# Pooled attention on one core: products with V in three blocks of 48 queries, two heads in the two halves of the PE's columns

## The chip, the cores and the metric

The kernel runs on one core of a Trainium2 chip (trn2). TensorE (PE) multiplies matrices, VectorE (DVE) and ScalarE (ACT) do elementwise work and move results out of the accumulators, GpSimd (POOL) does elementwise work in SBUF, and SyncE (SP) issues the DMAs. The metric is the device time of one execution in microseconds (us); the median of several runs is compared.

## The reference, cut to what matters

```python
q, k, v: (8 batches, 8 heads, 576 positions, 64)      # factor = 4, Sd = 576 // 4 = 144
q_d, k_d, v_d = mean over groups of 4 positions        # (8, 8, 144, 64)
out_d = softmax(q_d k_d^T / sqrt(64)) v_d              # pooled attention
out_up = np.repeat(out_d, 4, axis=2)
out_local = softmax over |i - j| < 4 of q k^T / sqrt(64), times v
x = (out_up + out_local), heads side by side           # (8, 576, 512)
xn = (x - mean) / sqrt(var + 1e-06) * g_ln
out = x + relu(xn @ w_ch1) @ w_ch2                     # 512 -> 2048 -> 512
```

The weights come as 64-bit floats and are read as pairs of 32-bit words.

## The kernel before, in words

One program holds both parts. The feed-forward part runs over 18 chunks of 256 tokens and, in each, over 8 pairs of 128-row blocks of the hidden layer: `up` (tile `h`, L1048), `relu` and `rest` (tiles `hh` on ACT, `hl` on DVE), `down` (tile `acc`, L1071). Each product is made of three passes over high and low parts of weights and activations. The weights are loaded by SP in 32 steps (tile `s`, L347 and L352: `s1_f` for the first matrix, `s2_f` for the second, f from 0 to 15) and split once into `hi` and `lo` by ACT (L359, L378) and DVE (tiles `cva`, L367 and L370, and `lo`, L383).

The attention part has 40 local windows (tiles `ls`, `lt`, `lv`; L587, L622, L643) and the pooled attention, which handles 4 heads at a time (`pooled_half`) and in it two pairs of heads (`pooled_pair`): 32 pairs in all, 4 of them in batch 0 (`own`, which gets its sums in another way) and 28 in the other batches. For one pair, both heads' queries stand in one block matrix `qbdg`, and the stages are: `turn_qk` (tile `gq`), `scores` (`gs`, L818, in three blocks of 48 queries a head), `largest`, `exps` (`ag`), `turn_a` (transposes into `gt`, L837, one for each half `kh` of the 144 keys), `turn_a_out` (ACT copies into `agt`, L847), `times_v` (products with V, tile `gv`, L854), `divided` (DVE, L861 to L871, tile `od`), and `keep` (DMA to the DRAM tile `ud`, L877), from where `load_up` (tile `up`, L917) reads it for the norm of the tokens. For the first seven windows and batch 0, other forms of some steps are used.

`times_v` makes, for each head h2 and each half qh of the 144 queries, a 72x65 block, summed over the two halves of the keys: 8 matrix products of 72 rows and 72 columns. A product of 32-bit floats is two passes on the PE, so that is 16 passes a pair, and 512 in all.

The order of everything is fixed before the program runs. `Plan.add` takes an engine, a duration, dependencies and a due time for every task; `Plan.order` plays the engines forward with these durations, and on each engine takes the task with the earliest due time among those that can start; the tasks are then written out in the order of their starts. Two kinds of numbers enter: the durations (1.04 for `times_v`) and the due times. `CHUNK` is the distance of chunks in due times, `chunk_at(c)` is `T0 + CHUNK * c` from the third chunk on, the times of windows and pooled pairs follow from it, and the weights are due at

```python
due = W0 + W_GAP * (f // 2) + 0.5 * (which - 1) + 1.0 * (f % 2)
```

or earlier, where a product that needs them is due earlier. Where the plan leaves the PE a gap in the first 150 us, `psa` writes extra products of the identity (L197) that only keep the PE running.

Of the kernel before, what the change touches and what calls it, by code (L numbers as in the profile page):

```python
# [9 lines left out]
F32 = mybir.dt.float32  # L10
# [4 lines left out]
ALU = mybir.AluOpType  # L15
# [7 lines left out]
class Plan:  # L23
# [14 lines left out]
    def add(self, eng, dur, fn, deps=(), due=0.0, take=(), give=(), lag=None, ahead=1e9, alt=None, kb=0):  # L38

        opts = {eng: (dur, fn, 0.0)}  # L40
        if alt is not None:
            opts[alt[0]] = alt[1:]
        t = SimpleNamespace(
            n=len(self.tasks), opts=opts, dur=dur, deps=[d for d in deps if d is not None],
            due=due, take=take, give=give, lag=lag, ahead=ahead, open=0.0, waits=0, eng=None, fn=None, kb=kb,
        )
        self.tasks.append(t)
        return t
# [91 lines left out]
def attention_then_ffn(  # L140
# [10 lines left out]
    nc = tc.nc  # L151

    P = 128
    B, H, S, D = q.shape
    DM = H * D
    w1, w2 = w1.bitcast(I32), w2.bitcast(I32)
    DFF = w1.shape[1] // 2
    FACTOR = 4
    SD = S // FACTOR
    GH = SD // 2  # L160
    GB = SD // 3
# [11 lines left out]
    NPE, NPB = 7, 1  # L173
# [11 lines left out]
    work = ctx.enter_context(tc.tile_pool(name="work", bufs=1))  # L185
    dram = ctx.enter_context(tc.tile_pool(name="dram", bufs=2, space=bass.MemoryType.DRAM))
    ps_a = ctx.enter_context(tc.tile_pool(name="ps_a", bufs=8, space=bass.MemoryType.PSUM))

    def unit(shape, name, dtype=F32, kind="u"):
        kind = kind if kind in SEP else "u"  # L190
        return work.tile(shape, dtype, tag=kind, bufs=SEP.get(kind, NU), name=name)

    def psa(name):
        p = ps_a.tile([P, 512], F32, tag="a", name=name)

        for _ in range(warm.pop() if warm else 0):
            nc.tensor.matmul(p[:, :P], lhsT=ident, rhs=ident, start=True, stop=True)  # L197
        return p
# [71 lines left out]

    T0 = 35
    C1 = 5
    CHUNK = 56
    PACE = CHUNK / NPR

    def chunk_at(c):
        return T0 + (C1 * c if c < 2 else CHUNK * c)

# [3 lines left out]
    def norm_at(n):  # L282
        c, j = divmod(n, TPC)
        return chunk_at(c) - 6.0 + 1.0 * j

    def window_of(n):
        b, s = divmod((n + 1) * P - 1, S)
        return b * NWIN + min(NWIN - 1, s // (2 * NQ))

    w_gap = CHUNK * S / T / NWIN  # L290
    w_base = min(norm_at(n) - 9.0 - window_of(n) * w_gap for n in range(2 * TPC, NTILE))
    g_base = min(norm_at(n) - 9.0 - (n * P + P - 1) // S * CHUNK * S / T for n in range(2 * TPC, NTILE))

# [5 lines left out]
    def pooled_at(b, pr):  # L299
        if b == 0:  # L300
            return norm_at(0) - B0G - B0G_GAP * (3 - pr)
        return g_base + b * CHUNK * S / T - (NPAIR - 1 - pr) * (CHUNK * S / T / NPAIR if b > 1 else G1)

# [2 lines left out]
    U_SPARE = 4  # L306
    NEARLY, EARLY = 2, 50
    G1, OFF0 = 6, 0.5
    W0, W_GAP = 40, 13
    plan = Plan({"u": NU, "stg": NSTG, "a": 8, **SEP}, {"a": 2, "u": U_SPARE})  # L310

    def rooms(*kinds):
# [6 lines left out]
    U, A, STG = (("u", 1),), (("a", 1),), (("stg", 1),)  # L319
    DMA, LAT, W_AHEAD, W_LAG = 0.5, 2.5, 40, 1.5  # L320
# [403 lines left out]
    ud, ud_done = {}, {}  # L724
    od, od_done = {}, []
# [8 lines left out]
    def pooled_half(b, hg):  # L734
# [41 lines left out]
        for pr in range(2):  # L776
            pooled_pair(b, hg, pr, x, ready)

    def pooled_pair(b, hg, pr, x, ready):
        add = plan.add  # L780
        i = 2 * b + hg
        due = pooled_at(b, 2 * hg + pr)
        y = SimpleNamespace(at={})
        own = b < NPB
        bd, vd = qbdg[pr], vds[hg]
# [47 lines left out]
        def turn_a(kh):  # L833
            y.pa = getattr(y, "pa", {})
            y.pa[kh] = psa(f"gt{i}_{pr}_{kh}")[:GH, : 2 * SD].rearrange("p (c h g) -> p c h g", c=3, h=2)
            for c in range(3):
                nc.tensor.transpose(  # L837
                    y.pa[kh][:, c].rearrange("p h g -> p (h g)"), y.a[:, c, kh * GH : (kh + 1) * GH],
                    ident[: 2 * GB, : 2 * GB],
                )  # L840

        def turn_a_out(kh):
            if own:
                y.at[kh] = unit([GH, 2, SD], f"agt{i}_{pr}_{kh}")
            else:
                y.at[kh] = work.tile([GH, 2, SD], F32, tag=f"agt{kh}", name=f"agt{i}_{pr}_{kh}")
            nc.scalar.copy(y.at[kh].rearrange("p h (c g) -> p c h g", c=3), y.pa[kh])  # L847

        def times_v():
            y.pv = psa(f"gv{i}_{pr}")[:GH, : 4 * (D + 1)].rearrange("p (q h e) -> p q h e", q=2, h=2)  # L850
            for h2 in range(2):
                for qh in range(2):
                    for kh in range(2):
                        nc.tensor.matmul(  # L854
                            y.pv[:, qh, h2], lhsT=y.at[kh][:, h2, qh * GH : (qh + 1) * GH],
                            rhs=vd[:, kh, 2 * pr + h2], start=kh == 0, stop=kh == 1,
                        )

        def divided():
            r = work.tile([GH, 2, 2], F32, tag="gr", bufs=4, name=f"gr{i}_{pr}")  # L860
            nc.vector.tensor_scalar(  # L861
                out=r, in0=y.pv[:, :, :, D], scalar1=1e-9, scalar2=float(FACTOR), op0=ALU.add, op1=ALU.mult
            )
            nc.vector.reciprocal(r, r)
            if b < NPB:
                if pr == 0:
                    od[hg] = unit([GH, 2, 2, 2 * D], f"od{i}")
                y.od = od[hg][:, :, pr].rearrange("p c (h d) -> p c h d", h=2)
            else:
                y.od = work.tile([GH, 2, 2, D], F32, tag="od", bufs=2, name=f"od{i}_{pr}")  # L870
            nc.vector.tensor_mul(y.od, y.pv[:, :, :, :D], r.unsqueeze(3).broadcast_to([GH, 2, 2, D]))  # L871
# [10 lines left out]
        if b < NPB:  # L882
            t = add("ACT", 0.43, arrange, ready["q"] + ready["k"] + [lastg.s[pr]], due - 8.0)
        else:
            t = add("PE", 0.25, turn_qk, ready["q"] + ready["k"], due - 8.0, take=A, give=(("u", 2),) if pr else ())
            t = add("ACT", 0.52, turn_qk_out, (t, lastg.s[pr]), due - 8.0, give=A)
        t = lastg.s[pr] = add(
            "PE", 0.73, scores, (t,), due - 6.0, take=A, give=(("u", 2),) if b < NPB and pr else ()
        )
        t = add("DVE", 0.7, largest, (t,), due - 5.0)  # L890
        ex = add("ACT", 0.79, exps, (t, None if own else lastg.t), due - 5.0, take=U if own else (), give=A)
        outs = []
        for kh in range(2):
            t = lastg.t = add("PE", 0.25, lambda kh=kh: turn_a(kh), (ex,), due - 3.0, take=A,
                                give=U if own and kh else ())
            outs.append(add("ACT", act(288), lambda kh=kh: turn_a_out(kh), (t, None if own else lastg.v), due - 3.0,
                            take=U if own else (), give=A))
        t = add("PE", 1.04, times_v, outs + ready["v"], due - 1.0, take=A, give=(("u", 2),) if own else ())
        lastg.v = lastg.vd[hg] = t
        t = add("DVE", 0.68, divided, (t,), due, take=U if b < NPB and pr == 0 else (), give=A)  # L900
        od_done.append(t)
        t = add("SP", 0.42, keep, (t,), due, lag=LAT)
        ud_done.setdefault(b, []).append(t)


# [265 lines left out]
```

## Time and profile before

| | |
|---|---|
| three runs | 1055.81, 1056.92, 1063.01 us; median 1056.92 |
| the profiled execution's own time | 1053.27 us |
| its span, first to last instruction | 1051.3 us |
| granted PE clock over the span | 0.995 |
| PE busy | 1034.3 us (98%) |
| DVE busy | 514.0 us (49%) |
| ACT busy | 309.8 us (29%) |
| POOL busy | 251.0 us (24%) |

A profile records one execution. Its durations are compared with its own time, 1053.27 us, of which 1.97 us lie outside the span. PE work is pipelined: the recorded durations of its passes overlap, so what a pass costs is read from one start to the next, not from the duration. "Granted clock" is the share of TensorE's full clock that was granted.

### The profile page before, as it was taken

Reading aid. Unit: us, or ns where it says so; the run is one execution under the profiler, and the core shown is the slowest. Engines: PE = TensorE matmul, PEld = TensorE weight load, DVE = VectorE, ACT = ScalarE, POOL = GpSimd, SP = SyncE. Lnnn points to the kernel's source line nnn. Section 1 sums busy time; section 2 is a strip of 40 time slices with the busy share of each in tenths; the row PEclk is TensorE's granted clock in tenths of the full one; section 3 lists DMA queues with packets and bytes.
Section 4 is the critical chain, followed back from the end, with each engine's and each line's share of the span. In section 5 each row is a group of like instructions: output and inputs, shape, how many; then the busy total and the mean of one; then the engine's idle time right before and its main releaser. Section 6 shows DMA issues by size and latency. Waiting matters only on the chain.

```text
span 1051.3 us, 24104 instructions
## 1 busy us (share of the span) xinstructions
PE 1034.3 (98%) x9450; PEld 928.9 (88%) x9450; DVE 514.0 (49%) x1301; ACT 309.8 (29%) x846; POOL 251.0 (24%) x272
## 2 busy tenths in 40 slices
PE   9999899999999999999999999999999999999998
PEld 8887798988899989989898989899989899888997
DVE  7799976343444435444434443544434444534211
ACT  6676533232212222221323222222221222221110
POOL 4213552214014320231404150141401300000000
PEclk9999999999999999999999999999999999999999
DMA  7897474434344534343434443253442443301000
GB/s 177 251 283 210 136 176 95 114 64 114 61 101 91 133 75 110 62 124 56 91 94 96 104 97 99 47 134 67 114 87 69 92 88 65 80 11 52 7 21 21
DMA packets 283702, 104.38 MB, mean 99 GB/s; under 512 B 229789, under 2 KB 270493, under 8 KB 283589
## 3 DMA queue, kind: packets, MB, share of 16 engines
q1 hardware_dynamic: 283589, 102.84, 40.8%
q8 instruction: 75, 1.23, 0.5%
q14 instruction: 38, 0.31, 0.1%
HBM read 82.58 MB, written 11.80 MB: 90 GB/s over the span
## 4 chain that ended last, share of the span: by engine, by line
PE 83%; DVE 6%; DMA 5%; SPq 2%; issue 1%; POOL 1%; ACT 1%; ACTq 0%; DVEq 0%; POOLq 0%
PE h L1048 34%; PE acc L1071 33%; PE gv L854 3%; DMA s<-in_moe_w_ch_dram 2%; PE gs L818 2%; PE lv L643 2%; PE ls L587 2%; DVE cva L370 2%; PE lt L622 1%; PE px L975 1%; PE gt L837 1%; DVE lo L383 1%; SPq L714 1%; DMA x<-xl 1%; DVE cva L367 1%
## 5 line engine op out<-in xcount | busy, mean ns | idle before, releaser
L1071 PE MATMUL acc<-hi,hl 128*128 128x512 f32 x576 | 237.2, 412 | 0.6 <-DVE hl L1059 0.5
L1071 PE MATMUL acc<-lo,hh 128*128 128x512 f32 x576 | 227.4, 395 | 0.0
L1071 PE MATMUL acc<-hi,hh 128*128 128x512 f32 x576 | 225.2, 391 | 0.0
L1059 DVE SCALAR_TENSOR_TENSOR hl<-h,hh 128x512 fp32r<-128x512 f32 x144 | 98.9, 687 | 250.7 <-ACT hh L1055 222.0
L1055 ACT ACTIVATE hh<-h 128x512 fp32r<-128x512 f32 x144 | 86.2, 599 | 430.3 <-PE h L1048 363.5
L1048 PE MATMUL h<-xh,lo 128*128 128x256 f32 x1152 | 193.6, 291 | 0.2 <-DVE lo L383 0.2
L1048 PE MATMUL h<-xh,hi 128*128 128x256 f32 x1152 | 185.2, 283 | 0.0
L1048 PE MATMUL h<-xlo,hi 128*128 128x256 f32 x1152 | 185.0, 283 | 0.0
L1048 PEld LDWEIGHTS h<-xh,lo 128*128 128x128 f32 x1152 | 169.0, 190 | 17.4 <-DVE lo L383 0.4
L1048 PEld LDWEIGHTS h<-xlo,hi 128*128 128x128 f32 x1152 | 158.9, 192 | 0.0
L1048 PEld LDWEIGHTS h<-xh,hi 128*128 128x128 f32 x1152 | 158.6, 191 | 0.0
L948 POOL TENSOR_TENSOR x<-x,up 128x512 f32<-128x512 f32 x32 | 41.2, 1287 | 386.3 <-DMA x<-xl 208.1
L1071 PEld LDWEIGHTS acc<-hi,hh 128*128 128x128 f32 x576 | 108.5, 188 | 25.0
L1071 PEld LDWEIGHTS acc<-hi,hl 128*128 128x128 f32 x576 | 109.2, 190 | 16.9 <-DVE hl L1059 1.2
L1071 PEld LDWEIGHTS acc<-lo,hh 128*128 128x128 f32 x576 | 109.5, 190 | 12.7 <-DVE lo L383 0.3
L982 ACT ACTIVATE xh<-px,gain 128x128 fp32r<-128x128 f32 x144 | 43.7, 372 | 72.7 <-PE px L975 42.4
L992 DVE SCALAR_TENSOR_TENSOR xlo<-px,gain,xh 128x128 fp32r<-128x128 f32 x144 | 43.1, 345 | 39.1 <-ACT xh L982 38.6
L1079 DVE SCALAR_TENSOR_TENSOR x<-acc,x 128x512 f32<-128x512 f32 x36 | 24.7, 689 | 39.8 <-PE acc L1071 39.8
L831 ACT ACTIVATE ag<-gs,gmx 96x144 f32<-96x144 f32 x96 | 29.0, 374 | 41.9 <-DVE gmx L823 34.4
L370 DVE SCALAR_TENSOR_TENSOR cva<-s,cva 128x256 int32<-128x256 int32 x64 | 40.0, 665 | 1.1
L854 PEld LDWEIGHTS gv<-vd,agt 72*72 72x72 f32 x512 | 37.1, 145 | 1.2
L854 PE MATMUL gv<-vd,agt 72*72 72x65 f32 x512 | 37.9, 228 | 0.0
(196 smaller groups left out, 1106.9 us busy)
## 6 DMA issues: line engine op xcount, KB each, us to landing
s<-in_moe_w_ch_dram SPq DMA_DIRECT2D x64, 256.0 KB
vwin<-in_v_dram SPq DMA_DIRECT2D x160, 64.0 KB
out_dram<-x SPq DMA_DIRECT2D x36, 256.0 KB
qr<-in_q_dram SPq DMA_DIRECT2D x264, 32.0 KB
kr<-in_k_dram SPq DMA_DIRECT2D x264, 32.0 KB
up<-ud SPq DMA_DIRECT2D x28, 256.0 KB
x<-xl SPq DMA_DIRECT2D x74, 42.0 KB
ud<-od SPq DMA_DIRECT2D x32, 72.0 KB
```

What stands on the lines that cost most here:

```text
L370: nc.vector.scalar_tensor_tensor(out=a, in0=x.raw[i].rearrange("p (n two) -> p n two", two=2)[:, :, 0], scalar=29, in1=a, op0=ALU.logical_ ...
L587: nc.tensor.matmul(x.ps[par][64 * h2 : 64 * h2 + 64, pr], lhsT=x.qt[hs, 2 * pr + h2], rhs=x.kt[hs, 2 * pr + h2], start=True, stop=True,)
L831: nc.scalar.activation(y.a[:, c], y.ps[:, c], AF.Exp, scale=POOLED_SCALE, bias=y.mx[:, c : c + 1])
L854: nc.tensor.matmul(y.pv[:, qh, h2], lhsT=y.at[kh][:, h2, qh * GH : (qh + 1) * GH], rhs=vd[:, kh, 2 * pr + h2], start=kh == 0, stop=kh == 1,)
L948: nc.gpsimd.tensor_add(xt[n], xt[n], x.up)
L982: nc.scalar.activation(xh[c][i][:, k, j * P : (j + 1) * P], pxt[n][:, kc], AF.Copy, scale=gain[:, kc : kc + 1])
L992: nc.vector.scalar_tensor_tensor(out=xlo[c][i][:, k, ts], in0=pxt[n][:, kc], scalar=gain[:, kc : kc + 1], in1=xh[c][i][:, k, ts].bitcast(F ...
L1048: nc.tensor.matmul(ph[c, p][:, fi], lhsT=wt[:, kc], rhs=xx[kc // 2][:, kc % 2], start=n == 0, stop=n == 3 * KC - 1)
L1055: nc.scalar.activation(hh[c, p], ph[c, p], AF.Relu)
L1059: nc.vector.scalar_tensor_tensor(out=hl[c, p].rearrange("p c t -> p (c t)"), in0=ph[c, p].rearrange("p c t -> p (c t)"), scalar=0.0, in1=h ...
L1071: nc.tensor.matmul(acc[c][j], lhsT=lt[:, fi, ts], rhs=rt, start=p == 0 and fi == 0 and n == 0, stop=p == NPR - 1 and fi == 1 and n == 2,)
L1079: nc.vector.scalar_tensor_tensor(out=x, in0=acc[c][j], scalar=1.0 + 2.0**-23, in1=x, op0=ALU.mult, op1=ALU.add)
```

## The change

For the 28 pairs of batches 1 to 7, `times_v_by_third` takes the place of `times_v`. The queries come in three blocks c of 48; head 0 of the pair gets output partitions 0 to 63 (48 of its own columns and 16 that belong to the next block and aren't used), head 1 partitions 64 to 111. `agt` is laid out flat, in the order in which the transposes leave it, so that a block's columns are contiguous. That makes 3 x 2 x 2 = 12 products of 64 or 48 columns a pair, in place of 8 of 72. `divided_by_third` handles 112 partitions x 192 elements in place of 72 x 256, and `keep_by_third` issues two DMAs in place of one, with rows of 64 elements in place of 128. Batch 0 stays as it was.

Three numbers of the plan change with it: the durations of these tasks (1.04 to 0.5 for the products, 0.68 to 0.6, 0.42 to 0.84), `CHUNK` from 56 to 55, and `W0` from 40 to 30. With these the plan writes out another order.

```diff
--- before.py
+++ after.py
@@ -270,7 +270,7 @@
 
     T0 = 35
     C1 = 5
-    CHUNK = 56
+    CHUNK = 55
     PACE = CHUNK / NPR
 
     def chunk_at(c):
@@ -306,7 +306,7 @@
     U_SPARE = 4
     NEARLY, EARLY = 2, 50
     G1, OFF0 = 6, 0.5
-    W0, W_GAP = 40, 13
+    W0, W_GAP = 30, 13
     plan = Plan({"u": NU, "stg": NSTG, "a": 8, **SEP}, {"a": 2, "u": U_SPARE})
 
     def rooms(*kinds):
@@ -842,9 +842,10 @@
         def turn_a_out(kh):
             if own:
                 y.at[kh] = unit([GH, 2, SD], f"agt{i}_{pr}_{kh}")
+                nc.scalar.copy(y.at[kh].rearrange("p h (c g) -> p c h g", c=3), y.pa[kh])
             else:
-                y.at[kh] = work.tile([GH, 2, SD], F32, tag=f"agt{kh}", name=f"agt{i}_{pr}_{kh}")
-            nc.scalar.copy(y.at[kh].rearrange("p h (c g) -> p c h g", c=3), y.pa[kh])
+                y.at[kh] = work.tile([GH, 6 * GB], F32, tag=f"agt{kh}", name=f"agt{i}_{pr}_{kh}")
+                nc.scalar.copy(y.at[kh], y.pa[kh].rearrange("p c h g -> p (c h g)"))
 
         def times_v():
             y.pv = psa(f"gv{i}_{pr}")[:GH, : 4 * (D + 1)].rearrange("p (q h e) -> p q h e", q=2, h=2)
@@ -855,6 +856,38 @@
                             y.pv[:, qh, h2], lhsT=y.at[kh][:, h2, qh * GH : (qh + 1) * GH],
                             rhs=vd[:, kh, 2 * pr + h2], start=kh == 0, stop=kh == 1,
                         )
+
+        def times_v_by_third():
+
+
+            y.pv = psa(f"gv{i}_{pr}")[: 64 + GB, : 3 * (D + 1)].rearrange("p (c e) -> p c e", c=3)
+            for c in range(3):
+                for kh in range(2):
+                    for h2 in range(2):
+                        m = GB if h2 else 64
+                        c0 = (2 * c + h2) * GB
+                        nc.tensor.matmul(
+                            y.pv[64 * h2 : 64 * h2 + m, c], lhsT=y.at[kh][:, c0 : c0 + m], rhs=vd[:, kh, 2 * pr + h2],
+                            start=kh == 0, stop=kh == 1,
+                        )
+
+        def divided_by_third():
+            r = work.tile([64 + GB, 3], F32, tag="gr", bufs=4, name=f"gr{i}_{pr}")
+            nc.vector.tensor_scalar(
+                out=r, in0=y.pv[:, :, D], scalar1=1e-9, scalar2=float(FACTOR), op0=ALU.add, op1=ALU.mult
+            )
+            nc.vector.reciprocal(r, r)
+            y.od = work.tile([64 + GB, 3, D], F32, tag="od", bufs=2, name=f"od{i}_{pr}")
+            nc.vector.tensor_mul(y.od, y.pv[:, :, :D], r.unsqueeze(2).broadcast_to([64 + GB, 3, D]))
+
+        def keep_by_third():
+            if b not in ud:
+                ud[b] = dram.tile([SD, DM], F32, tag="ud", name=f"ud{b}")
+            for h2 in range(2):
+                c0 = (4 * hg + 2 * pr + h2) * D
+                nc.sync.dma_start(
+                    ud[b].rearrange("(c g) e -> g c e", c=3)[:, :, c0 : c0 + D], y.od[64 * h2 : 64 * h2 + GB]
+                )
 
         def divided():
             r = work.tile([GH, 2, 2], F32, tag="gr", bufs=4, name=f"gr{i}_{pr}")
@@ -895,11 +928,11 @@
                                 give=U if own and kh else ())
             outs.append(add("ACT", act(288), lambda kh=kh: turn_a_out(kh), (t, None if own else lastg.v), due - 3.0,
                             take=U if own else (), give=A))
-        t = add("PE", 1.04, times_v, outs + ready["v"], due - 1.0, take=A, give=(("u", 2),) if own else ())
+        t = add("PE", 1.04 if own else 0.5, times_v if own else times_v_by_third, outs + ready["v"], due - 1.0, take=A, give=(("u", 2),) if own else ())
         lastg.v = lastg.vd[hg] = t
-        t = add("DVE", 0.68, divided, (t,), due, take=U if b < NPB and pr == 0 else (), give=A)
+        t = add("DVE", 0.6, divided if own else divided_by_third, (t,), due, take=U if b < NPB and pr == 0 else (), give=A)
         od_done.append(t)
-        t = add("SP", 0.42, keep, (t,), due, lag=LAT)
+        t = add("SP", 0.42 if own else 0.84, keep if own else keep_by_third, (t,), due, lag=LAT)
         ud_done.setdefault(b, []).append(t)
 
 
```

On the PE, at the products of one pair (`gv2_0`: batch 1, first half of the heads, first pair; `vd` holds the pooled v, the two `agt` the two halves of the keys), before:

```order
L1071 MATMUL acc0_1_1301<-hi2_7_1776,hl0_3_1871 128x512
L1071 MATMUL acc0_1_1301<-lo2_7_1788,hh0_3_1847 128x512
L1071 MATMUL acc0_1_1301<-hi2_7_1776,hh0_3_1847 128x512
L854 MATMUL gv2_0_1984<-vd0_82,agt2_0_0_1964 72x65
L854 MATMUL gv2_0_1984<-vd0_82,agt2_0_1_1966 72x65
...
L818 MATMUL gs2_1_2000<-ktg2_1_1980,qbdg1_81 96x144 x3
```

and now (the two rows that follow the first two of `gv` are the same for the other half of the keys; these four come three times):

```order
L1104 MATMUL acc0_1_1340<-hi2_7_1686,hh0_3_1875 128x512
L869 MATMUL gv2_0_2010<-vd0_82,agt2_0_0_1994 64x65
L869 MATMUL gv2_0_2010<-vd0_82,agt2_0_0_1994 48x65
L869 MATMUL gv2_0_2010<-vd0_82,agt2_0_1_1998 64x65
L869 MATMUL gv2_0_2010<-vd0_82,agt2_0_1_1998 48x65
...
L818 MATMUL gs2_1_2026<-ktg2_1_1976,qbdg1_81 96x144 x3
```

Eight products of one form became twelve, which go to the lower and the upper half of the columns in turn; the work on both sides of them is of the same kind as before.

On SP's queue, at the first weights (`s1` and `s2` are the two weight matrices' raw words, `qn5`, `kn5` and `vwin0` belong to local window 5, `ud0` to batch 0), one piece of the difference:

```order
 L347 DMA s1_0_1_586<-in_moe_w_ch1_dram 128x2x256
-L347 DMA s1_1_0_608<-in_moe_w_ch1_dram 128x2x256
-L347 DMA s1_1_1_609<-in_moe_w_ch1_dram 128x2x256
-L487 DMA qn5_634<-in_q_dram 64x8x64 x2
+L352 DMA s2_0_0_608<-in_moe_w_ch2_dram 128x512
+L352 DMA s2_0_1_609<-in_moe_w_ch2_dram 128x512
+L347 DMA s1_1_0_634<-in_moe_w_ch1_dram 128x2x256
+L347 DMA s1_1_1_635<-in_moe_w_ch1_dram 128x2x256
 L502 DMA vwin0_76<-in_v_dram 64x4x64 x4
-L487 DMA kn5_742<-in_k_dram 64x8x64 x2
-L877 DMA ud0_787<-od0_772 72x2x128 x2
-L352 DMA s2_0_0_812<-in_moe_w_ch2_dram 128x512
```

The second matrix's first block moved ahead of the first matrix's second block, of window 5's q and k and of batch 0's store.

On DVE, from the second block's `lo1_1` to the first `hl` of chunk 0 (`cva` and `lo` are the splitting of weights, `xlo` the low part of the normed tokens, `lmx5` the maximum in window 5, `hl0_0` the low part of the hidden layer in chunk 0, pair 0), before:

```order
L383 TENSOR_TENSOR lo1_1_1155<-cva1_1_838,hi1_1_1114 128x512
L992 SCALAR_TENSOR_TENSOR xlo1_1_1157<-px2_1087,gain_75,xh1_1_1107 128x128 x2
L367 TENSOR_SCALAR cva2_0_932<-cva2_0_932 128x512
L370 SCALAR_TENSOR_TENSOR cva2_0_932<-s2_0_0_812,cva2_0_932 128x256
L370 SCALAR_TENSOR_TENSOR cva2_0_932<-s2_0_1_813,cva2_0_932 128x256
L992 SCALAR_TENSOR_TENSOR xlo1_0_1149<-px3_1163,gain_75,xh1_0_1102 128x128 x2
L992 SCALAR_TENSOR_TENSOR xlo1_1_1157<-px3_1163,gain_75,xh1_1_1107 128x128 x2
L598 TENSOR_REDUCE lmx5_1228<-ls5_0_1193 128x4
L598 TENSOR_REDUCE lmx5_1228<-ls5_1_1194 128x4
L600 TENSOR_SCALAR lmx5_1228<-lmx5_1228 128x8
L1059 SCALAR_TENSOR_TENSOR hl0_0_1250<-h0_0_1122,hh0_0_1213 128x512
```

and now:

```order
L383 TENSOR_TENSOR lo2_0_1193<-cva2_0_839,hi2_0_1106 128x512
L383 TENSOR_TENSOR lo1_1_1198<-cva1_1_869,hi1_1_1122 128x512
L1025 SCALAR_TENSOR_TENSOR xlo1_1_1209<-px2_1090,gain_75,xh1_1_1114 128x128 x2
L383 TENSOR_TENSOR lo2_1_1226<-cva2_1_873,hi2_1_1132 128x512
L1025 SCALAR_TENSOR_TENSOR xlo1_0_1183<-px3_1200,gain_75,xh1_0_1101 128x128 x2
L598 TENSOR_REDUCE lmx5_1244<-ls5_0_1134 128x4
L598 TENSOR_REDUCE lmx5_1244<-ls5_1_1143 128x4
L600 TENSOR_SCALAR lmx5_1244<-lmx5_1244 128x8
L1025 SCALAR_TENSOR_TENSOR xlo1_1_1209<-px3_1200,gain_75,xh1_1_1114 128x128 x2
L1092 SCALAR_TENSOR_TENSOR hl0_0_1270<-h0_0_1169,hh0_0_1257 128x512
```

The splitting of the second matrix's first two blocks is over before `hl0_0` now; before, `lo2_0` and all of block `2_1` came after it.

## Rows read from the trace of the kernel before

**Rows 1.** The page's first part: the span, and the PE's busy time.
```profile
span 1051.3 us, 24104 instructions
...
PE 1034.3 (98%) x9450; PEld 928.9 (88%) x9450; DVE 514.0 (49%) x1301; ACT 309.8 (29%) x846; POOL 251.0 (24%) x272
```

**Rows 2.** Windows: length, busy us of PE, PEld, DVE, ACT, POOL, clock, DMA, GB/s.
```profile
250.00:300.00 50.00, 50.00 (x461) 45.09 (x461) 20.51 (x58) 15.24 (x47) 7.05 (x8) 1.00 0.41 80
...
900.00:1000.00 100.00, 100.00 (x814) 90.05 (x813) 35.99 (x96) 18.20 (x42) 7.34 (x8) 1.00 0.13 36
```

**Rows 3.** The same view in the stretch in which weights are split.
```profile
30.00:50.00 20.00, 20.00 (x260) 17.57 (x259) 15.06 (x56) 12.41 (x39) 2.24 (x4) 1.00 0.84 237
...
65.00:80.00 15.00, 15.00 (x118) 13.04 (x109) 14.49 (x30) 10.06 (x28) 4.55 (x4) 1.00 0.97 312
...
120.00:140.00 20.00, 17.52 (x130) 15.51 (x129) 19.59 (x36) 9.29 (x26) 8.51 (x8) 0.91 0.52 121
```

**Rows 4.** Waits of the PE over the span: total us, times, longest.
```profile
PE gt L837 <- ACT ag L831: 3.2, 2, 2.1
PE lv L643 <- ACT at L629: 2.2, 1, 2.2
PE gs L818 <- ACT ktg L804: 1.6, 4, 0.9
...
PE gs L818 <- DVE hl L1059: 1.4, 1, 1.4
PE lt L622 <- ACT la L617: 1.2, 1, 1.2
```

**Rows 5.** Windows around three of these waits.
```profile
88.00:98.00 10.00, 7.81 (x68) 6.75 (x67) 9.83 (x22) 7.58 (x21) 2.48 (x3) 0.83 0.58 171
...
127.00:139.00 12.00, 9.73 (x65) 8.28 (x64) 11.69 (x26) 5.83 (x18) 3.48 (x4) 0.86 0.70 155
...
220.00:232.00 12.00, 9.90 (x89) 8.73 (x88) 6.59 (x19) 7.18 (x26) 2.26 (x3) 0.86 0.31 59
```

**Rows 6.** PE's timeline at one pair's products: start, length in us, what, passes.
```profile
495.54 0.64 PE L1048 MATMUL h<-xlo,hi 128*128 128x256 f32 x4
496.01 0.40 PE L1071 MATMUL acc<-hi,hl 128*128 128x512 f32 x1
496.25 0.40 PE L1071 MATMUL acc<-lo,hh 128*128 128x512 f32 x1
...
514.16 0.64 PE L1048 MATMUL h<-xlo,hi 128*128 128x256 f32 x4
514.63 1.20 PE L854 MATMUL gv<-vd,agt 72*72 72x65 f32 x16
...
515.95 0.39 PE L1071 MATMUL acc<-lo,hh 128*128 128x512 f32 x1
```

**Rows 7.** The same view at a local window's products, in quarters of the array.
```profile
497.18 0.39 PE L1071 MATMUL acc<-hi,hh 128*128 128x512 f32 x1
...
497.88 0.64 PE L1048 MATMUL h<-xh,hi 128*128 128x256 f32 x4
...
500.43 0.40 PE L1071 MATMUL acc<-hi,hh 128*128 128x512 f32 x1
500.76 0.70 PE L643 MATMUL lv<-vwin,at 64*64 64x65 f32 x32
...
501.96 0.64 PE L1048 MATMUL h<-xh,hi 128*128 128x256 f32 x4
```

**Rows 8.** The same view at batch 0's transposes, in halves of the columns.
```profile
6.12 0.72 PE L428 MATMUL lk<-ident,ko 80*64 80x80 f32 x16
...
8.89 0.72 PE L428 MATMUL lq<-ident,qo 80*64 80x80 f32 x16
```

**Rows 9.** Tile views: DVE's product into od, and its store.
```profile
L871 DVE TENSOR_TENSOR od<-gv,gr x32: 420/420/421, 32.6 to 880.5; 72x256 f32<-72x256 f32 x32
L877 SPq DMA_DIRECT2D ud<-od x32: 298/365/627, 35.5 to 883.2; - x32
```

## The prediction

> **What bounds the kernel now.** I read the page's first part first: the PE is busy for 1034.3 of 1051.3 us [rows 1]. Then the windows: of the eight from 250 us to 1000 us the first and the last stand here, in which it is busy all the time [rows 2], as in the others but for 1.4 us, so there every pass that goes or comes moves the end by its own price. The exception is the time before 250 us. The list of the PE's waits has 8.2 us there in all (3.2 behind `ag`, 2.2 behind `at`, 1.6 behind `ktg`, 1.2 behind `la`), and one of 1.4 us behind `hl` near 786 us [rows 4]. All four early releasers are ACT's, and the stretch from 65 to 140 us, in which most of this time lies, has a DVE that is full: 14.49 of 15 us and 19.59 of 20 us, while between 30 and 50 us it still had 5 us free [rows 3]. ACT's queue holds the rounding of weights, which waits for DVE's `cva`, and the attention's copies stand behind it. Around three of the waits the granted clock is 0.83, 0.86 and 0.86 over 10, 12 and 12 us [rows 5], so part of each window ran at 1.2 GHz instead of 2.4: each costs 1.7 us of full speed (0.17 x 10, 0.14 x 12) on top of the wait. So this is a PE-bound kernel with some 13 us (8.2 + 3 x 1.7) of early losses. The change touches both sides: passes on the PE, and the order of the early weights.
>
> **The products with V, before.** A stretch without them goes from the start of the last group of `h` to the second `acc` in 496.25 - 495.54 = 0.71 us; with the 16 passes of `gv` in between it takes 515.95 - 514.16 = 1.79 us [rows 6]. One pair costs 1.08 us. `gv` starts 0.47 us after the `h` group, and without it `acc` starts 0.47 us after `h`: these passes use the whole array, like their neighbours, and enter without delay. From `gv`'s start to the next group there are 1.01 us, 63 ns a pass.
>
> **The products with V, after.** 24 passes, alternately in the two halves of the columns. Two things set their price: whether the halves run at once, and what it costs to go from the whole array to the halved one and back.
>
> The first is shown by batch 0's transposes, whose form is nearly the same: 80 rows, so all row groups of the array, 64 columns, and the two heads in the two halves of the columns in turn. Five groups of 16 passes take 8.89 - 6.12 = 2.77 us [rows 8], 0.554 us a group, 35 ns a pass and 69 ns for two. A `gv` pass by itself takes 63 ns with fewer columns streamed. So the halves do run at once. With 65 columns streamed in place of 80 and the same 64 loaded, I scale by (64 + 65) / (64 + 80) to 0.062 us for two passes; 12 such rounds make 0.74 us.
>
> The second comes from the local windows, whose `lv` products run in quarters of the array, four passes at a time. Without them the way from the last `acc` to the second group of `h` takes 497.88 - 497.18 = 0.70 us, with them 501.96 - 500.43 = 1.53 us [rows 7], so 32 passes, which are 8 rounds, cost 0.83 us. Here the first pass starts 0.33 us after the last `acc`, where one `acc` follows another in 0.24 us [rows 6]: going in waits. At 0.062 us a round, 8 rounds are 0.50 us and 0.33 us is left for going in and out. I take the same 0.33 us for the halved array, as the nearest row: 0.74 + 0.33 = 1.07 us a pair, against 1.08. With rounds as long as in the transposes (0.069), `lv` leaves 0.28 us and a pair costs 0.83 + 0.28 = 1.11 us; with rounds as short as the 48-column head's would be, (48 + 65) / 144 x 0.069 = 0.054 us, it is 0.65 + 0.40 = 1.05 us. Over 28 pairs: -0.8 to +0.8 us, and I take **-0.3 us**. What overlap gives, the change of mode takes.
>
> **DVE, ACT, SP.** `od` takes 420 ns for 256 elements a partition [rows 9]; with 192 it lies between 315 ns (in proportion) and 420, so at most 28 x 0.105 = 2.9 us of DVE time go, nearly all of it behind 140 us, where DVE has room: nothing on the path. ACT copies the same 288 elements. `keep` issues two DMAs of 298 to 627 ns each in place of one [rows 9]: 8 to 18 us more of SP's time over some 770 us, behind which the next q and k loads stand. The plan has these up to 45 us ahead of their due times (`AHEAD`), and what a late load can cost is the 1.4 us wait at 786 us [rows 4]. So between nothing and 3 us (two such waits); I take nothing, because that wait occurs once in 800 us. The order has 34 identity products in the plan's gaps in place of 28. Six of them are 12 passes of the whole array with 128 columns, between `gv`'s 63 ns and the 0.24 us of an `acc` with 512 [rows 6], so 0.8 to 2.9 us, and nothing where the PE would wait anyway; near the lower end, and with some of them under waits, I take **+0.5 us**.
>
> **The early order.** `W0` and `CHUNK` pull the weights forward: on SP the second matrix's first block now stands before the first matrix's second block and before window 5's q and k, and on DVE all of blocks 0 and 1 are split before the first `hl` of chunk 0. The splitting itself isn't less, and between 65 and 140 us DVE is full with or without that. What can be won is the 5 us that DVE had free between 30 and 50 us [rows 3]: work done there shortens the full stretch. What can be lost is that `hl0_0` stands behind more splitting, and with it the first `down`. DMA transport is no free resource either: its share is 0.84 and 0.97 in these stretches [rows 3]. I take one early wait of about 2.2 us with its drop of the clock as gone: 2.2 + 1.7 = **-3.9 us**. Bounds: all early losses gone, -13 us, or as many waits added, at 3.9 us each, up to two, +8 us. This is the least certain term, and it decides the sign.
>
> **After 250 us** `CHUNK` 55 in place of 56 stretches nothing: due times only rank tasks, and a PE that is busy all the time takes the same work in a slightly different order.
>
> **Sum.** -0.3 + 0.5 - 3.9 = -3.7 us: 1053.27 becomes 1049.6 us for an execution like the profiled one. That execution is 3.65 us below the median of the runs, 1056.92, so against the median the time is 1056.92 - 3.7 = **1053.2 us**, 0.35% less.
>
> **Rivals.**
>
> The halves don't run at once. Then 24 passes of one tile stand in a row; at 0.062 us they take 1.49 us instead of 0.74, so 0.75 us more a pair, 21 us in all: 1074 us, slower. For it: the two halves share all their rows and stream the same kind of operand. Against it: the transposes in [rows 8] have just this arrangement and take 35 ns a pass. It decides if a round in the new `gv` takes over 0.1 us. The Trainium skill has a rule that would give this result: "TensorE: Matmul & The Clock Gate", Part 3, "The mechanism", says that a weight load overlaps products under way only when it goes to other row groups, and here both halves use the same ones. By that rule alone the transposes could not run at 35 ns a pass, so the trace speaks against it. Chance 0.04.
>
> The change of mode is free, because half columns differ less from the whole array than quarters do. Then a pair costs 0.74 us, 0.34 less, 9.5 us in all, and with the other terms 1044.0 us: faster by over 1%. The trace shows no entry into the halved array between two full groups in the busy stretch, so it can't be ruled out, but every entry into quarters pays. The Trainium skill's "TensorEngine Tiling (Array Packing)", "Theoretical Speedup", gives up to twofold for outputs of at most 64 columns, which is what this rival would need; its "Key Properties" has a drain at each change of mode, and the 0.33 us agree with that. Chance 0.06.
>
> The early losses dissolve, because DVE takes half of the splitting off the full stretch: -10 us and more, so 1047 us or less. For it: DMA of weights and DVE's `cva` and `lo` are what the waits go back to. Against it: DVE's work in 65 to 140 us stays, and only 5 us were free before. Chance 0.10, of which 0.06 beyond 1%.
>
> The early order gets worse: three more waits of the kind in [rows 5], since `hl0_0` and its successors stand behind the splitting, at 3.9 us each, without the gain: +12 us, 1069 us. Chance 0.04.
>
> **How the numbers follow.** The forecast case, with the early term anywhere between -8 and +8 us, keeps 0.76. From these: faster by over 1% (10.6 us, about what a measurement of this kernel can tell from no change) 0.12, slower by over 1% 0.08, within 1% 0.80. The range for 8 times in 10 goes from 1045 us (12 of the 13 us of early losses gone) to 1062 us (one more early wait, +3.9, and one more late one, +1.4, with nothing gained).
>
> **What would show it.** In the changed kernel's trace a pair's `gv` should start 0.1 us late after its neighbour, take about 31 ns a pass and cost 1.05 to 1.11 us in all between `h` and `acc`; if it costs 0.75, the second rival holds, if 1.8, the first. The sum of the PE's early waits should be about 6 us with two drops of the clock. DVE's `od` should take under 420 ns, and the time from 250 us on should be as before within 1 us. The prediction is wrong if the early waits change by more than 8 us, or if the order brings back waits behind DMAs after 250 us.

## The result and the profile after

The changed kernel takes 1063.99 us (median of 20 runs, 1057.16 to 1068.39) against 1055.28 us for the kernel before beside it (20 runs, 1050.59 to 1063.01): a ratio of 1.0078, interval 1.0058 to 1.0097. So it is slower by 8.7 us, where 3.7 us less were predicted, and 2 us beyond the range. It stays within 1%, but the interval excludes no change, and the sign was wrong.

The profiled execution took 1068.39 us. Its page:

```profile
span 1066.7 us, 24637 instructions
...
PE 1042.1 (98%) x9686; PEld 930.5 (87%) x9686; DVE 508.2 (48%) x1297; ACT 312.3 (29%) x862; POOL 251.1 (24%) x272
```

**The products** do what was predicted. The PE's timeline of this execution, one stretch without and one with `gv` (columns as in [rows 6]):

```profile
521.52 0.64 PE L1081 MATMUL h<-xlo,hi 128*128 128x256 f32 x4
522.00 0.40 PE L1104 MATMUL acc<-hi,hl 128*128 128x512 f32 x1
522.23 0.40 PE L1104 MATMUL acc<-lo,hh 128*128 128x512 f32 x1
...
524.87 0.64 PE L1081 MATMUL h<-xlo,hi 128*128 128x256 f32 x4
525.43 0.91 PE L869 MATMUL gv<-vd,agt 72*64 72x65 f32 x24
526.28 0.50 PE L1104 MATMUL acc<-hi,hl 128*128 128x512 f32 x1
526.61 0.39 PE L1104 MATMUL acc<-lo,hh 128*128 128x512 f32 x1
```

From the last group of `h` to the second `acc` it is 0.71 us without and 1.74 us with `gv`: a pair costs 1.03 us, before 1.08 [rows 6]. `gv` starts 0.56 us after `h`, where its neighbours and the old `gv` take 0.47 to 0.48, and from its start to the next group there are 0.85 us for 24 passes and the way out. The tile views of `od` and `ud`, beside [rows 9]:

```profile
L881 DVE TENSOR_TENSOR od<-gv,gr x28: 357/358/360, 128.6 to 895.9; 112x192 f32<-112x192 f32 x28
```
```profile
L888 SPq DMA_DIRECT2D ud<-od x56: 309/434/1082, 129.0 to 899.7; - x56
```

DVE is faster by 62 ns a pair; SP issues twice as many stores, none of them shorter. The window from 900 to 1000 us is full, as in [rows 2]:

```profile
900.00:1000.00 100.00, 100.00 (x865) 89.57 (x863) 40.33 (x107) 19.84 (x48) 9.20 (x10) 1.00 0.18 47
```

**The start of this execution is an exception.** In the windows view, 0 to 30 us, the first row is the execution just shown, the second the same kernel profiled again (`e17_after_again`, below):

```profile
0.00:30.00 30.00, 28.50 (x364) 26.84 (x365) 14.79 (x35) 12.35 (x32) 16.04 (x36) 1.00 0.83 189
```
```profile
0.00:30.00 30.00, 27.06 (x526) 24.71 (x530) 19.82 (x49) 19.48 (x56) 14.54 (x35) 1.00 0.78 169
```

Busier, with 364 passes in place of 526: the passes themselves were slow. The row says 1.00 for the clock, but the transposes tell otherwise; first execution, then second:

```profile
L428 PE MATMUL lq<-ident,qo x128: 340/341/396, 5.2 to 22.9; 80*64 80x80 f32 x128
```
```profile
L428 PE MATMUL lq<-ident,qo x128: 232/233/396, 5.2 to 17.1; 80*64 80x80 f32 x128
```

The last of them starts 5.8 us later. These passes ran as slowly as at 1.2 GHz: 16 of them take 1.07 us here (6.34 to 7.41 us) under a row of 1.00, and 1.12 us (17.99 to 19.11 us) in `e16_chunk54_w0_40`, below, whose row reads 0.50 from 15 to 20 us. The same start, 28.50 us with 364 passes, stands in `e6_store_by_half`, which has the order of before, so it isn't the new order's. The second execution, 1062.33 us, stands nearer to the median, so I read the rest there. Where it loses is seen beside the same kernel with W0 at 40 (`e4_w0_40`, 1054.15 us), whose span is 8.7 us shorter. Two windows, of `e17_after_again` and of `e4_w0_40`:

```profile
30.00:65.00 35.00, 32.90 (x416) 29.12 (x406) 30.11 (x98) 25.84 (x80) 3.99 (x6) 1.00 0.86 244
...
780.00:810.00 30.00, 25.50 (x200) 22.32 (x200) 11.90 (x30) 6.93 (x21) 1.84 (x2) 0.94 0.41 88
```
```profile
30.00:65.00 35.00, 34.85 (x411) 31.01 (x400) 30.16 (x98) 25.07 (x77) 2.21 (x4) 1.00 0.87 250
...
780.00:810.00 30.00, 30.00 (x275) 26.89 (x275) 15.18 (x39) 7.97 (x23) 0.69 (x2) 1.00 0.47 101
```

In the first window 34.85 - 32.90 = 1.95 us are missing. In the second 4.5 us are idle, and a granted clock of 0.94 over 30 us (0.66 from 791 to 796 us, so part of it at 1.2 GHz, right behind the wait) takes 1.8 more. Together 8.2 of the 8.7 us; the other stretches differ by up to 2 us either way.

**Near 55 us.** ACT's timeline of `e17_after_again`, then that of `e4_w0_40`:

```profile
55.26 0.60 ACT L524 COPY lqt<-lq 128x512 f32<-128x512 f32 x1
55.84 0.62 ACT L378 CAST hi<-cva 128x512 fp32r<-128x512 f32 x1
56.37 0.58 ACT L524 COPY lkt<-lk 128x512 f32<-128x512 f32 x1
```
```profile
54.96 0.62 ACT L524 COPY lqt<-lq 128x512 f32<-128x512 f32 x1
55.44 0.62 ACT L524 COPY lkt<-lk 128x512 f32<-128x512 f32 x1
```

With W0 at 30 one of the weights' `hi` stands between the two copies of the attention, and on the PE `ls`, which needs them, now stands ahead of the first `h` (in `e4_w0_40` it starts at 59.21 us, behind it). The PE's timelines, in the same order:

```profile
55.31 0.38 PE L559 MATMUL ls<-mask_b,ident_b 128*128 128x256 bf16 x2
57.00 0.69 PE L573 MATMUL ls<-lkt,lqt 64*64 64x64 f32 x32 [1.30 <-ACT lkt L524]
...
57.87 0.72 PE L1081 MATMUL h<-xh,lo 128*128 128x256 f32 x4
```
```profile
53.24 1.95 PE L197 MATMUL h<-ident 128*128 128x128 f32 x16
55.08 0.71 PE L1081 MATMUL h<-xh,lo 128*128 128x256 f32 x4
```

The first `h` comes 2.8 us later.

**Near 790 us.** The list of the PE's waits of `e17_after_again`, columns as in [rows 4]:

```profile
PE lt L622 <- ACT la L617: 5.2, 2, 3.9
PE px L1008 <- DVE xn L999: 5.0, 2, 4.5
...
PE gt L837 <- ACT ag L831: 1.7, 1, 1.7
...
PE lv L643 <- ACT at L629: 1.4, 1, 1.4
...
PE gs L818 <- ACT ktg L804: 1.2, 2, 0.9
```

The waits behind `ag`, `at` and `ktg` fell from 7.0 to 4.3 us, that behind `la` grew from 1.2 to 5.2 (in `e4_w0_40` too, to 4.8, and that order loses nothing). The one behind `xn` is new in this size (0.3 before), and the chain of waits says what it hangs on:

```profile
788.27 0.63 SPq L714
...
788.95 2.13 DMA x<-xl
...
791.26 0.56 DVE xn L999
...
791.95 1.09 PE px L1008 x4
```

L714 moves the attention's result `xl` into the token tile `x`: ten DMAs here, 0.8 us of SP's time each. SP's timeline of `e17_after_again`, then of `e4_w0_40`:

```profile
774.96 2.75 SPq L478 DMA_DIRECT2D kr<-in_k_dram  x4
777.90 0.59 SPq L950 DMA_DIRECT2D up<-ud  x1
778.54 2.95 SPq L496 DMA_DIRECT2D vwin<-in_v_dram  x4
781.59 8.16 SPq L714 DMA_DIRECT2D x<-xl  x10
```
```profile
772.18 2.40 SPq L478 DMA_DIRECT2D qr<-in_q_dram  x4
775.00 0.56 SPq L950 DMA_DIRECT2D up<-ud  x1
775.65 8.52 SPq L714 DMA_DIRECT2D x<-xl  x10
```

SP works with hardly a gap in both, and comes to the ten issues 5.9 us later with W0 at 30. The PE is late there too, by 3.75 us (the `px` ahead of the one that waits starts at 784.03 us against 780.28), so SP has lost 2.2 us against it. The rest of the wait is no lack of data. DVE's timeline of `e17_after_again`:

```profile
786.14 0.70 DVE L989 BATCH_NORM_STATS2 st<-x 128x6 f32<-128x512 f32 x1 [4.74 <-DMA x<-xl]
...
791.26 0.55 DVE L999 TENSOR_SCALAR xn<-x,mv 128x512 f32<-128x512 f32 x1 [2.75 <-DMA x<-xl]
```

`st` reads the same tile `x` as `xn`, so `x` was complete by 786.14 us; `xn` still waits until the last of the ten transfers has landed (788.95 + 2.13 us). In `e4_w0_40` `xn` follows `st` by 1.86 us, without a wait; at that distance the PE would have waited 1.2 us in place of 4.5, an estimate. In kernel.py `xn` and `xl` are both `unit` tiles, which share one set of buffers, so `xn` may have to wait until `xl` has been read and its buffer is free; no run tests that.

### The profile page after: what moved, and what is told of

Same layout as the page of the kernel before. It is cut to its first block, busy times and chain, and to the rows that moved or that the text cites. A ratio compares the mean times of both kernels' runs of the same rounds, so it can differ in the third digit from the quotient of the medians.

```text
span 1066.7 us, 24637 instructions
## 1 busy us (share of the span) xinstructions
PE 1042.1 (98%) x9686; PEld 930.5 (87%) x9686; DVE 508.2 (48%) x1297; ACT 312.3 (29%) x862; POOL 251.1 (24%) x272
## 4 chain that ended last, share of the span: by engine, by line
PE 88%; DVE 5%; DMA 3%; issue 2%; SPq 1%; ACT 1%; POOL 0%; DVEq 0%; ACTq 0%; POOLq 0%
PE h L1081 35%; PE acc L1104 34%; PE lv L643 2%; PE gs L818 2%; PE ls L587 2%; PE gv L869 2%; PE lt L622 2%; PE px L1008 2%; DVE lo L383 1%; PE gt L837 1%; DMA x<-xl 1%; DVE cva L370 1%; DMA s<-in_moe_w_ch_dram 1%; PE lq L428 1%; PE lk L428 1%
## 5 line engine op out<-in xcount | busy, mean ns | idle before, releaser
L989 DVE BATCH_NORM_STATS2 st<-x 128x6 f32<-128x512 f32 x32 | 21.9, 684 | 35.3 <-POOL x L981 26.1
L822 DVE TENSOR_REDUCE gmx<-gs 96x3 f32<-96x432 f32 x32 | 19.2, 600 | 39.7 <-PE gs L818 39.7
L995 POOL TENSOR_TENSOR mv<-mv,neg_half 128x1 f32<-128x1 f32 x36 | 19.7, 548 | 76.0 <-DVE mv L992 54.3
```

The source lines that it names most:

```text
L989: nc.vector.bn_stats(st, x.up if by_pe else xt[n])
```

## The experiments

All are timed in five rounds against the kernel before on the same chip. Settings: CHUNK, W0, the plan's durations, the code of products and stores.

| run | setting | median us | ratio, interval |
|---|---|---|---|
| e1_products_only | 56, 40, old, new: before's order | 1064.94 | 1.0097, 1.0069 to 1.0124 |
| e2_order_only | 55, 30, new, old: the new order | 1060.23 | 1.0053, 1.0021 to 1.0084 |
| e3_chunk56 | 56, 30, new, new | 1065.86 | 1.0104, 1.0068 to 1.0140 |
| e4_w0_40 | 55, 40, new, new | 1054.21 | 0.9992, 0.9961 to 1.0024 |
| e11_chunk56_w0_40 | 56, 40, new, new | 1056.04 | 1.0022, 0.9993 to 1.0052 |
| e12_w0_35 | 55, 35, new, new | 1062.22 | 1.0071, 1.0043 to 1.0098 |
| e5_store_by_head | before, two stores of 64-element rows | 1059.02 | 1.0036, 1.0006 to 1.0066 |
| e6_store_by_half | before, two stores of 128-element rows | 1060.41 | 1.0044, 1.0022 to 1.0067 |
| e7_second_on_act | e1, second store issued by ACT | 1057.69 | 1.0016, 0.9993 to 1.0039 |
| e8_after_second_on_act | after, second store by ACT | 1060.91 | 1.0066, 1.0038 to 1.0094 |
| e9_w0_40_second_on_act | e4, second store by ACT | 1052.87 | 1.0003, 0.9974 to 1.0033 |
| e10_stores_on_act | before, its 28 stores by ACT | 1053.69 | 0.9994, 0.9958 to 1.0030 |
| e13_before_w0_30 | before, W0 30 alone | 1058.82 | 1.0056, 1.0033 to 1.0080 |
| e14_second_matrix_30 | after, W0 30 for the second matrix, 40 for the first | 1062.40 | 1.0076, 1.0049 to 1.0103 |
| e15_first_matrix_30 | after, W0 30 for the first, 40 for the second | 1059.57 | 1.0026, 0.9995 to 1.0058 |
| e16_chunk54_w0_40 | 54, 40, new, new | 1059.26 | 1.0038, 1.0015 to 1.0060 |
| e17_after_again | after, unchanged | 1064.48 | 1.0094, 1.0061 to 1.0127 |
| e18_x_on_pool | after, L714's DMAs issued by POOL | 1051.38 | 1.0003, 0.9973 to 1.0033 |

**Products, order, W0, CHUNK apart.**

> New products, division and stores, with the plan's numbers of before, so in before's order. If the order is the cause (theory A), this is faster than before by 28 x (1.083 - 1.034) = 1.4 us, ratio 0.998 to 1.000, with the waits of before near 91, 118, 131, 223 and 787 us. If the new stores or products are the cause (theory B: two DMA issues for one make SP's queue late, and loads behind it), this is slower by 6 to 10 us, ratio 1.006 to 1.010, and the wait near 787 us grows from 1.4 to about 4 us.

> Old products, division and stores, in the changed kernel's order (CHUNK 55, W0 30, the new durations). Theory A: slower than before by 9 to 10 us, ratio 1.008 to 1.010, with waits near 100, 121, 149, 233 and 797 us as in the changed kernel. Theory B: as before, ratio 0.998 to 1.002.

> The changed kernel with CHUNK 56. If the shorter distance of chunks is what puts norms and attention too early for their loads (theory A1), most of the loss goes: ratio 0.998 to 1.002, the wait near 797 us gone or back to 1.4 us. If it is the earlier weights (A2), it stays: ratio 1.006 to 1.010, and the waits before 150 us stay at some 8 us.

> The changed kernel with W0 40. A2 (earlier weights): the waits before 150 us fall from some 8 us to 5, ratio 1.000 to 1.004. A1 (distance of chunks): the waits near 233 and 797 us stay at 4 to 5 us each, ratio 1.005 to 1.009.

> The new code with CHUNK 56 and W0 40, and only the plan's durations of the new tasks (0.5, 0.6 and 0.84 in place of 1.04, 0.68 and 0.42). If the plan must know that a store takes SP twice as long (theory C), this is faster than the new code with the old durations (1.0097): ratio 0.998 to 1.003. If W0 and CHUNK don't matter by themselves and an order is good or bad by chance (theory L), anything from 0.998 to 1.011.

> The changed kernel with W0 35, between 30 (1.008) and 40 (0.999). If earlier weights cost in themselves (A2), ratio 1.002 to 1.006. Theory L: it need not lie between.

```diff
-    CHUNK = 55
+    CHUNK = 56
-    W0, W_GAP = 30, 13
+    W0, W_GAP = 40, 13
```

Each run takes one or both of these lines, or 35. W0 from 30 to 40 gives back 8.6 per mille at CHUNK 55 (1.0078 to 0.9992) and 8.2 at 56 (1.0104 to 1.0022): it is the main cost, and 35 is no better than 30. CHUNK 55 is 2.6 to 3 per mille better than 56, within the intervals. The two halves of the change do not add up: the new code in before's order loses 9.7 per mille, the old code in the new order 5.3, together 7.8; e2's 5.3 lies between what the two theories expected. The new code at W0 40 in an order that knows its durations costs 2.2 at CHUNK 56 (e11), in before's order 9.7 (e1): the difference is the order alone. e1 runs the very products that after runs, and e7, with the same products in the same order, comes to 1.0016, so e1's loss lies elsewhere.

**The second store.**

> The kernel before, with each of the 28 stores issued as two DMAs, one for each head (rows of 64 elements, as in the changed kernel). If the stores are what slows the new products in the old order (theory B), this is slower than before by 9 to 11 us, ratio 1.008 to 1.011, with longer waits near 223 and 787 us. If the products, the copy or the division do it (theory P), ratio 0.998 to 1.002.

> The same with one DMA for each half of the queries: two issues, but rows of 128 elements and as many of them as before. If the second issue costs (B1: SP's time), ratio 1.006 to 1.011 as in the run by head. If the short rows cost (B2), 0.998 to 1.002. Theory P: 0.998 to 1.002.

> New products in the old order with the second head's store issued by ACT in place of SP: the same rows, SP's issues as before. B1: back to before or 1 us less, ratio 0.997 to 1.002, the late waits back to 1.4 us. B2 or P: 1.007 to 1.011 as with both on SP.

> The changed kernel with the second head's store on ACT. B1 and the order's own loss of 0.5 per cent: ratio 1.002 to 1.005. If stores and order don't add up but each has its own luck: anywhere from 0.998 to 1.008, and the waits will show other places.

> The changed kernel with W0 40 (0.999 with both stores on SP) and the second head's store on ACT. If every issue taken from SP gives time back (theory B1, at any order), ratio 0.994 to 0.998. If SP's time counts only where an order leaves it no slack (B3), and the order with W0 40 has some, 0.997 to 1.001.

> The kernel before with the 28 stores issued by ACT, so 28 issues fewer on SP, some 11 us of its time. B1: as much faster as the doubled store was slower, ratio 0.995 to 0.998. B3: 0.998 to 1.002.

```diff
-            nc.sync.dma_start(
-                ud[b].rearrange("(c g) e -> g c e", c=2)[:, :, c0 : c0 + 2 * D],
-                y.od.rearrange("p c h d -> p c (h d)"),
-            )
+            to = ud[b].rearrange("(c g) e -> g c e", c=2)
...
+            for h2 in range(2):
+                nc.sync.dma_start(to[:, :, c0 + h2 * D : c0 + (h2 + 1) * D], y.od[:, :, h2])
```
```diff
-                nc.sync.dma_start(
+                (nc.scalar if h2 else nc.sync).dma_start(
```

The first diff is e5's; e6 splits by the half of the queries in place of the head, and e7 to e9 have the second. A second DMA costs the kernel before 3.6 or 4.4 per mille whatever the length of the rows, less than the 6 to 11 expected. In e1 issuing it from ACT gives back 8 per mille (1.0097 to 1.0016), the transfers being the same, so it is SP's issue that costs; the late waits did not go back to 1.4 us as expected, but from 7.2 us behind `xn` after 250 us to one of 3.2. In the changed kernel the same move gives 1.2 per mille (e8), within the intervals. In e4, whose plan counts both issues, the same move gives nothing (0.9992 and 1.0003), and neither does taking 28 issues away from before's SP (0.9994). So SP's time counts where the order leaves it no slack. The Trainium skill, "DMA: Bandwidth & Descriptors", section "Issuing engines are not separate DMA queues", says that issuing from several engines saves only the issuing sequencer's time, usually small beside the DMA. The first half agrees; here that small time (0.43 us in the row of `ud`, 28 times, beside 2 us in which `x` lands) was worth some 8 us.

**Whose early weights.**

> The kernel before with W0 at 30 and nothing else changed (old products, one store a pair, CHUNK 56, old durations). Theory: pulling the weights forward costs 8 to 9 us by itself, in any surroundings, so this takes 1062 to 1065 us, a ratio of 1.006 to 1.010. Rival: it costs only together with the new durations or the second store; then 1.000 (1.003 at most).

> The changed kernel with W0 at 30 for the second matrix alone, 40 for the first. Theory: the loss comes from the second matrix's blocks, whose loads and splitting are put some 10 us ahead of the first matrix's, so it stays: 1.006 to 1.009. Rival: the first matrix's blocks, or the two together, cause it; then 0.999 to 1.002, as with W0 at 40 for both.

> The changed kernel with W0 at 30 for the first matrix alone, 40 for the second. Theory: the first matrix's early blocks are due early anyway, so nothing is lost: 0.998 to 1.002. Rival: the loss is the first matrix's: 1.006 to 1.009.

> The changed kernel with W0 at 40 and CHUNK at 54. It is another order that pulls no weights forward. Theory: an order as such costs nothing, only the early weights do: 0.996 to 1.002. Rival: any order other than the one before was tuned on loses something: 1.004 or more.

```diff
-        due = W0 + W_GAP * (f // 2) + 0.5 * (which - 1) + 1.0 * (f % 2)
+        due = (40 if which == 1 else W0) + W_GAP * (f // 2) + 0.5 * (which - 1) + 1.0 * (f % 2)
```

The diff is e14's; e15 has the two numbers the other way round. W0 at 30 costs the kernel before 5.6 per mille by itself, with no other edit, less than the 6 to 10 expected. But not near 790 us: in e13's profiled execution (1060.61 us) that window is full, and the PE's largest wait is behind `la`, both times before 250 us:

```profile
780.00:810.00 30.00, 30.00 (x249) 27.09 (x251) 13.35 (x34) 8.13 (x23) 1.84 (x2) 1.00 0.47 102
```
```profile
PE lt L622 <- ACT la L617: 10.0, 2, 5.2
```

Given to the second matrix alone it brings the whole loss (1.0076), as the theory had it; to the first alone 1.0026, between the two expectations, with an interval that reaches no change. In e14 the windows read as in `e17_after_again`:

```profile
30.00:65.00 35.00, 31.68 (x379) 28.13 (x379) 28.89 (x94) 24.97 (x77) 3.54 (x6) 1.00 0.84 237
...
780.00:810.00 30.00, 26.40 (x240) 23.08 (x239) 13.02 (x33) 7.46 (x22) 1.84 (x2) 0.94 0.43 97
```

e16 went against the theory: an order that pulls no weights forward loses 3.8 per mille as well. So I see two parts. Every order with the second matrix at 30 loses 5.3 to 10.4 per mille (after, e2, e3, e8, e13, e14; e18, which takes issues off SP, apart); those with it at 40 whose plan counts both stores lie between -0.8 and 3.8 (e4, e9, e11, e15, e16), which looks like a lottery that each new order draws. The late wait belongs to the lottery: after 250 us the PE waits behind `xn` for 5.1 us in e16, whose weights are not early, and not at all in e13. Where W0 35 loses its 7.1 per mille isn't known: e12's profiled execution, the fastest of its runs (1055.19 us), has neither loss (34.84 of 35 us, 30.00 of 30).

**What the late wait is.**

> The changed kernel once more, unchanged, for a second profiled execution: in the first one the products of the first 28 us ran at half clock, which cost some 10 us and hides the rest. Theory: without that start the execution loses its time at 30 to 65 us (PE less busy than the 34.5 us of before by 1 to 3 us), at the waits up to 235 us and at 4 us or more near 790 us, with three or more drops of the clock (mean 0.99). Rival: the slow start is what the change costs; then it is there again.

> The changed kernel (W0 30, CHUNK 55, order unchanged) with the DMAs of L714 (x from xl, those of the windows that are not moved by PE) issued by POOL in place of SP, which takes some 0.8 us of SP's queue away for each. Theory: the late wait near 790 us is SP's queue reaching these ten issues 6 us too late; with them on another queue the PE's wait behind xn (4.5 us in the second profile) falls under 1 us, 780 to 810 us holds 29 us or more of PE work, and some 6 of the 8 us come back: 1.001 to 1.004. Rival: the wait has another cause (xl itself is late, or the DMA transport is); then the wait stays and the ratio is 1.007 to 1.010. A third outcome: POOL's issuing is slower and its own elementwise work becomes late; then other waits, behind POOL, appear and the ratio is 1.008 or more.

```diff
                 for h2 in range(2):
                     for r1, r2 in ((0, cut), (cut, m)) if cut else ((0, m),):
-                        nc.sync.dma_start(
+                        nc.gpsimd.dma_start(
```

e17 showed the slow start to be no part of the change. e18 leaves the order alone and takes 262 issues off SP. The tile views of `x` in e17 and in e18, and the windows of e18:

```profile
L714 SPq DMA_DIRECT2D x<-xl x262: 610/811/1657, 185.5 to 983.5; - x131
```
```profile
L714 POOL DMA_DIRECT2D x<-xl x262: 520/585/729, 188.0 to 971.1; - x131
```
```profile
30.00:65.00 35.00, 31.98 (x382) 28.21 (x381) 29.74 (x96) 25.50 (x79) 3.57 (x6) 1.00 0.83 238
...
150.00:250.00 100.00, 100.00 (x916) 90.01 (x915) 49.13 (x119) 28.64 (x91) 42.54 (x52) 1.00 0.45 105
...
780.00:810.00 30.00, 29.83 (x269) 26.42 (x269) 14.79 (x38) 7.71 (x21) 8.16 (x13) 1.00 0.29 73
```

The wait near 790 us is gone, the one near 225 us too, and the time falls by 9 per mille, from 1.0094 to 1.0003, more than the 1.001 to 1.004 expected. The wait near 225 us stands in the kernel before as well [rows 5], so part of this gain is none of the change's own loss. The same 100 us in e17, then in the kernel before:

```profile
150.00:250.00 100.00, 96.10 (x876) 85.89 (x875) 44.97 (x111) 26.67 (x82) 25.59 (x26) 0.98 0.41 89
```
```profile
150.00:250.00 100.00, 97.39 (x855) 87.30 (x854) 50.34 (x123) 28.28 (x89) 32.79 (x33) 0.98 0.44 104
```

The early loss stays (31.98 us from 30 to 65 us), as it must, since L714 begins at 188 us. So the late wait near 790 us is a matter of late issues, not of a late `xl` (in e17 it is written by 776.0 us, and the first of the ten issues starts at 781.59).

## Why the prediction was wrong, point by point

**The products** were right in mechanism and nearly in size: the halves run at once (24 passes and the way out in 0.85 us; one after another they would take 1.49 us), going in waits 0.09 us where 0.1 was forecast, and a pair costs 1.03 us where 1.07 was forecast, so 28 x 0.05 = 1.4 us are won in place of 0.3. The rival by which the halves don't run at once fell. So did the free change of mode: a pair at 0.74 us was not seen.

**The early order** was the step that failed: "one early wait of about 2.2 us with its drop of the clock as gone". This term of -3.9 us measured +9 (8.6 per mille between e4 and after, which differ in W0 alone). What I named as the possible loss, attention and `h` behind more splitting, came true near 55 us, at 2 us; of the four early waits named, three fell by 2.7 us in all, as hoped, and the fourth grew by 4.0 (in the kernel before with W0 30, whose loss is early, by 8.8). I weighed the 5 us that DVE had free and not ACT's queue, in which the weights' `hi` stands between copies the PE waits for. And I looked for the cost of W0 at the start alone.

**After 250 us** `CHUNK` "stretches nothing: due times only rank tasks": this failed with it. The larger part of the changed kernel's loss, 6.3 us of 8.2 in the second profile, lies near 790 us, and with it came the sign that the prediction had named, waits behind DMAs after 250 us. Nothing there has to do with weights; W0 changed which issues stand ahead of L714 on SP (e4 against e17 differ in W0 alone). How the greedy order carries a shift of 10 us in early due times to there was not followed.

**The stores** were taken at nothing, "because that wait occurs once in 800 us". In the new order with W0 40 that held. In before's order a second issue costs 4 us (e5, e6). What it delays is not the loads of q and k, as I wrote, but the moves of L714. I put the price of a late transfer at the 1.4 us wait in [rows 4]; with the drop of the clock behind it, it is 6.3 us. That wait, whose chain in the profile before begins with 3.67 us of `DMA x<-xl` at 779.81 us, I read now as the mark of a queue without slack: the PE waits behind `xn` for 4.5 us there in the second profile, 8.7 us at three places in e1, and not at all in e4.

**DVE and ACT** as forecast: `od` takes 358 ns, between 315 and 420 [rows 9], and nothing follows from it.

Open: why the second store costs 8 per mille with the new products and 4 with the old ones in the same order; and what e18's edit would give the kernel before, or W0 at 40. Neither was run, so beyond the wait near 225 us it isn't known how much of e18's gain is the change's own loss undone and how much is new. That W0 is the main cost is shown; how it decides between an early and a late loss is not.

## What to carry to other kernels

A number that sets an order is not local: look for its price on the queue with the least slack anywhere in the program, here SP, whose issues stand back to back, and not only where the number acts. A single late wait of 1.4 us behind a transfer was the sign of such a queue here; price it with the drop of the clock that a longer one brought (a clock of 1.00 over 30 us with the 1.4 us wait, 0.94 with 4.5 us). And when an edit adds issues to such a queue, either tell the planner or issue them from an idle engine, and test the edit and the order apart.

## What the runs showed of the hardware that was not expected

Passes in two column halves, which share all their rows, run at once also between full groups, and the change of mode takes about as much as it gives: with the 0.74 us that the transposes [rows 8] make for 24 passes, an estimate, 1.03 - 0.74 = 0.29 us of a pair are going in and out. POOL issued the DMAs of L714 in 585 ns where SP took 811. And a profile can hide a slow clock: in the first execution the granted clock reads 1.00 over 30 us in which a transpose took 341 ns in place of 233, as it does in e16 where the row says 0.50; the durations of a known pass tell, the clock's row doesn't.
